# Q and K weights first on ScalarE's queue; Q projected once, its norm rows in a bank of their own

## The chip, the cores and the metric

The kernel runs on one core of one Trainium2 chip. The metric is device time in microseconds: the median of the runs of one program, lower is better. The profile comes from one further execution, which has a time of its own.

## The reference

There are two branches over the same sequence, mixed by a gate. One is softmax attention with 16 heads of 28 dimensions over 2048 tokens of width 448. The other is a spectral filter: a 2-D real FFT of x, a product with a complex weight, and the inverse FFT.

```python
def reference(A_x, A_wqkv, A_wo, B_x, B_w_r, B_w_i, gate_w):
    # A: qkv = x @ wqkv, 16 heads of 28; p = softmax(q k^T * 28**-0.5); a = (p v) @ wo
    # B: X = rfft2(x) over sequence and width; b = irfft2(X * (w_r + 1j * w_i))
    x = A_x                                            # [1, 2048, 448]
    g = _sigmoid((x * gate_w).sum(-1, keepdims=True))
    a = _A_ref(x, A_wqkv, A_wo)
    b = _B_ref(x, B_w_r, B_w_i)
    return g * a + (1 - g) * b
```

As the kernel computes it, both branches read the same x.

## The kernel before

The program is a list of operations (`Op`), each with an engine, an estimated duration, what it depends on and a key. A planner that ran beforehand put all of them into one order. That order is stored as the compressed constant `PLAN`, with the PSUM bank of each background item and a list of the operations that are moved to VectorE. `plan()` unpacks it and `issue()` emits the operations in that order, so the order of every engine's instructions, and of every queue's transfers, is fixed when the kernel is built. Each engine works through its instructions strictly in order. Numbers from 60000 up in the list stand for fillers: four matmuls over a tile of zeros into `pvb`, which change no result and which the planner puts where it expects TensorE to wait. PSUM has 8 banks: `psA` has three, `psB` two, `pvb` one, and `bg` two, which the background items share.

Attention works in 16 rounds (`plan_steps`): 4 groups of 4 heads, by 4 blocks of 512 queries. In each round the scores of a key tile are computed transposed, k by q, for four heads side by side. Most of them go through ScalarE's exponential (line 962), three units of 512 columns from `psA` and then two from `psB`, in turn, 307 times in all; `ring` keeps the results until `pvb` has summed them against the values. For the other key tiles, VectorE (line 997) and GpSimd or VectorE (line 1009, the phase operations) form the exponential from bits. The norms of q and k enter the scores as two more rows of q and k: a row with -0.5 times the sum of squares on one side stands against a row of ones on the other. The constants `selq` and `selk` pick those rows in a matmul over the squares in `sq`.

The FFT branch, the projections of later groups and the output run as background between the scores: the forward FFT, 16 products (`CS` and `Wg` are loaded for each), the inverse FFT and the output tiles.

The head (`head`, from line 499) is what must be done before the first scores. It loads the first 512 tokens of x in two halves of two tiles (`dx`, 224 KB each, into `xtok`) and the weights of group 0 of Q and K (`raws`, 98 KB each, into `X`). Two queues issue loads: SyncE's (SP) and ScalarE's (ACT). GpSimd prepares constants and the zero columns of the padded weights (`padset`); ScalarE copies the raw weights into them (`padcopy`, line 494). While x is on its way, `NWARM` = 14 matmuls over zeros keep TensorE busy. Then x is transposed in four chunks c of 112 columns, each in a PSUM bank of its own (psA, psB, pvb and a background bank), and evicted to `xT` (lines 555 and 557), psB by ScalarE and the others by VectorE. Each projection is four matmuls over these chunks.

Q's first block is projected twice, into psA (`qa`), from which the squares are taken, and into pvb (`qb`), to which the norm row is added (`mq`) before pvb is evicted as q. The squares of `qa` are shared: 320 columns on ScalarE (line 582), 192 on VectorE (lines 584 and 586). The eviction is shared as well: 256 columns on VectorE (line 595), 256 on ScalarE (line 593). For K, the first `KA` = 256 columns follow the same scheme (`ka`, `kb`, `mk`; evicted by VectorE, line 597), the other 256 come behind (`kc`, `kd`, `mc`). Where two engines read one bank, the layer that builds the program makes them do so in turn. All matmuls carry the helper's line, 417, and all transposes 425.

## Time and profile before

| | us |
|---|---|
| median of 3 runs | 386.98 (386.85 to 387.02) |
| profiled execution, its time | 387.57 |
| its span, first to last instruction | 385.8 |
| TensorE busy | 370.4 |
| ScalarE busy | 366.1 |
| VectorE busy | 339.9 |
| GpSimd busy | 226.1 |

Busy times are of the span. A busy TensorE need not be at its peak: matmuls overlap, and each counts until its modelled end, so two matmuls that start 0.2 us apart may each show 0.38. In the timeline a row gives the start, the duration, the engine, the line, the operation with output and input, and in brackets how long the engine was idle before and what ended that. Rows merge equal instructions that follow each other (x14); "128*113 128x128" are the weights and the moving operand. `X` is the tile of raw weights, `wpq` and `wpk` the padded weights of Q and K, `ring` the result of the exponential. SPq and ACTq are the engines' queues issuing transfers.

### The profile page before, as it was taken

To read this page: it belongs to the slowest core of one execution; us is meant where nothing else is said; L and a number is where in the kernel's file an instruction comes from. 1 tells how busy PE (TensorE), PEld (TensorE's weight loads), DVE (VectorE), ACT (ScalarE), POOL (GpSimd) and SP (SyncE) were. 2 spreads that over 40 slices of the span, in tenths; PEclk is the share of its full clock that TensorE was granted. 3 is DMA by queue.
4 is the path that set the end of the run, shared out by engine and by line. 5 is a ranking of instruction groups with operands and counts; after the bars stand their busy time and mean duration, and the time that the engine had idled before them with its cause. 6 is when DMAs were issued, how large, how long until landed. Compare 5 with 4: busy or idle time off the path is not lost.

```text
span 385.8 us, 12111 instructions
## 1 busy us (share of the span) xinstructions
PE 370.4 (96%) x4978; PEld 142.3 (37%) x4978; DVE 339.9 (88%) x559; ACT 366.1 (95%) x333; POOL 226.1 (59%) x235
## 2 busy tenths in 40 slices
PE   7999999999999999999899999999999999999996
PEld 4643323334343334333233334332334323333343
DVE  1768989998999999999999999999999999977534
ACT  3899999999999999999999999999999999999993
POOL 4133686344566677878796776766557853454500
PEclk9999999999999999999999999999999999999999
DMA  8451000001230013233323212211123120030211
GB/s 212 99 147 39 3 2 2 14 6 45 55 108 4 2 51 79 72 73 99 71 79 70 48 31 75 67 41 25 46 76 103 51 66 14 4 82 26 56 37 62
DMA packets 31811, 21.63 MB, mean 56 GB/s; under 512 B 16572, under 2 KB 29596, under 8 KB 31756
## 3 DMA queue, kind: packets, MB, share of 16 engines
q1 hardware_dynamic: 30876, 20.41, 20.5%
q8 instruction: 39, 0.64, 0.7%
q10 hardware_dynamic: 880, 0.44, 0.4%
q14 instruction: 16, 0.13, 0.1%
HBM read 14.97 MB, written 1.97 MB: 44 GB/s over the span
## 4 chain that ended last, share of the span: by engine, by line
PE 63%; DVE 17%; ACT 5%; DMA 5%; issue 4%; POOL 2%; SPq 1%; ACTq 0%; DVEq 0%; POOLq 0%
PE bg L417 29%; PE pvb L417 20%; DVE pd L997 7%; PE psA L417 7%; PE psB L417 6%; ACT ring L962 5%; DVE pd L1009 3%; DMA CS<-cCS 2%; DVE X L1301 2%; POOL pd L1009 1%; SPq L400 1%; DMA X<-in_A_wqkv_dram 1%; DMA xtok<-Ab 1%; DMA Rb<-rsc 1%; DVE tt L1258 1%
## 5 line engine op out<-in xcount | busy, mean ns | idle before, releaser
L962 ACT ACTIVATE ring<-psA 128x1536 bf16<-128x1536 f32 x154 | 228.8, 1486 | 4.2 <-PE psA L417 3.1
L1009 POOL TENSOR_SCALAR pd<-pd 128x2048 uint16<-128x2048 uint16 x83 | 157.1, 1901 | 81.8 <-DVE pd L1009 47.1
L962 ACT ACTIVATE ring<-psB 128x1024 bf16<-128x1024 f32 x153 | 162.5, 1062 | 2.1 <-PE psB L417 1.6
L997 DVE TENSOR_SCALAR pd<-bg 128x512 uint16<-128x512 f32 x236 | 156.0, 683 | 9.0 <-PE bg L417 5.1
L417 PE MATMUL bg<-q,k 32*128 32x512 bf16 x236 | 88.0, 379 | 3.4 <-DVE pd L997 0.9
L417 PE MATMUL pvb<-pd,vd 128*32 128x512 bf16 x944 | 85.5, 384 | 0.3 <-DVE pvs L1078 0.2
L417 PEld LDWEIGHTS <-k 32*128 32x128 bf16 x1024 | 37.4, 91 | 106.7 <-issue 100.6
L417 PE MATMUL pvb<-ring,vw 128*32 128x512 bf16 x768 | 71.1, 384 | 0.0
L1009 DVE TENSOR_SCALAR pd<-pd 128x2048 uint16<-128x2048 uint16 x94 | 65.7, 715 | 1.3
L417 PE MATMUL psA<-q,k 32*128 32x512 bf16 x474 | 64.1, 383 | 0.7 <-ACT ring L962 0.6
L417 PE MATMUL psB<-q,k 32*128 32x512 bf16 x314 | 62.4, 383 | 1.1 <-ACT ring L962 0.5
L417 PEld LDWEIGHTS <-vd 128*32 128x32 bf16 x944 | 22.9, 94 | 36.1 <-issue 31.1
L417 PEld LDWEIGHTS <-vw 128*32 128x32 bf16 x788 | 19.5, 94 | 31.4 <-issue 26.6
L1089 POOL TENSOR_TENSOR q<-pvs,Rb 128x512 bf16<-128x512 f32 x15 | 19.2, 1277 | 13.4 <-DVE pd L1009 5.2
L417 PEld LDWEIGHTS <-xT 112*128 112x128 bf16 (+1 forms) x512 | 19.6, 97 | 9.8 <-issue 6.4
L1258 DVE TENSOR_TENSOR tt<-bg,Wg 128x900 bf16<-128x900 f32 x16 | 17.4, 1091 | 2.0 <-PE bg L417 1.5
L417 PE MATMUL bg<-xT,wpk 112*32 112x512 bf16 (+2 forms) x252 | 18.3, 376 | 0.3 <-DVE pd L997 0.2
L875 POOL TENSOR_TENSOR vd<-vraw,wg 128x448 bf16<-128x448 f32 x16 | 15.0, 942 | 4.9 <-DVE pd L1009 4.2
L417 PE MATMUL bg<-xT,wpq 112*32 112x512 bf16 (+1 forms) x240 | 17.7, 382 | 0.2 <-DVE pd L997 0.2
L417 PE MATMUL bg<-wo,q 128*32 128x448 bf16 x236 | 17.5, 354 | 0.0
L1157 DVE CAST fin<-bg 128x448 bf16<-128x448 f32 x12 | 7.5, 624 | 10.8 <-PE bg L417 8.2
L417 PE MATMUL bg<-Bd,X 113*32 113x448 bf16 x240 | 16.8, 355 | 0.0
(125 smaller groups left out, 321.0 us busy)
## 6 DMA issues: line engine op xcount, KB each, us to landing
Rb<-rsc SPq DMA_DIRECT2D x60, 64.0 KB
CS<-cCS SPq DMA_DIRECT2D x16, 192.0 KB
Wg<-in_B_w_i_dram SPq DMA_DIRECT2D x64, 28.1 KB
xtok<-Ab SPq DMA_DIRECT2D x16, 112.5 KB
V<-xtok SPq DMA_DIRECT2D x16, 112.5 KB
xtok<-in_A_x_dram SPq DMA_DIRECT2D x3, 448.0 KB
out_dram<-fin SPq DMA_DIRECT2D x12, 112.0 KB
Wg<-in_B_w_r_dram SPq DMA_DIRECT2D x32, 28.1 KB
```

Source lines behind the costliest of these rows:

```text
L400: self.pin(e.dma_start(out=out() if callable(out) else out, in_=in_() if callable(in_) else in_))
L417: self.pin(self.nc.tensor.matmul(out, lhsT=lhsT, rhs=rhs, start=start, stop=stop, **kw))
L875: self.pin(nc.gpsimd.tensor_tensor(out=self.vd[g][:, f, :, :, 0:DH], in0=src, in1=wv, op=ALU.mult))
L962: self.pin(nc.scalar.activation(out=home[:, u0:u0 + len(st), :], in_=slot[:, 0:len(st), :], func=ACT.Exp, scale=LN2 / UNITS))
L997: self.pin(nc.vector.tensor_scalar(out=self.pd[y.bank][:, s, :].bitcast(U16), in0=self.bgi(it), scalar1=127 * UNITS, scalar2=0.0, op0=ALU. ...
L1009: self.pin(e.tensor_scalar(out=fl(self.pd[z.bank]), in0=fl(self.pd[y.bank]), scalar1=float(PHASE[f]), scalar2=1.0, op0=ALU.add, op1=ALU.mult))
L1089: e = self.pool(1.24, lambda: self.pin(nc.gpsimd.tensor_tensor(out=dst, in0=pvs[:], in1=self.Rb[:], op=ALU.mult)), ds, kk)
L1157: e = self.dve(0.55, lambda: self.pin(V.tensor_copy(out=fin, in_=bank())), [ops[-1], self.fdma[t % 2]], key, **a)
L1258: self.pin(nc.vector.tensor_tensor(out=tt[:], in0=free_dims(self.bgi(it), [[0, 2], [F, 2], [1, F]]), in1=free_dims(Wg[:], [[F, 2], [F, 2], ...
L1301: self.pin(nc.vector.tensor_tensor(out=free_dims(self.zt[0:FN], [[128, 4], [1, 128]], 512 * t), in0=self.bgi(it)[0:FN, :].rearrange("p (a ...
```

## The change

- ScalarE's queue issues Q's weights and then K's; SyncE's queue issues both halves of x. Before, each queue issued one half of x and then one of the two weights.
- The transposes of all four chunks of the first half of x stand ahead of those of the second half, and in the new order the last of them stand ahead of Q's projection.
- Q's first block is projected once, into psA. ScalarE evicts it to q with the scale CQ (`qc`); VectorE squares q in SBUF (`sq`); the norm rows go alone into pvb (`mq`, now opening its bank), and VectorE adds pvb to q in one operation (`qe`).
- ScalarE still squares the first 256 columns of K, and now also evicts them (`self.k0`). The other 256 columns stay on VectorE.
- The warm-up matmuls write another bank of psA.
- `PLAN` is new as a whole. What it makes of the order: TensorE has 12 warm-ups, the transposes of the first half for psB, a warm-up, psA, a warm-up, pvb, then the second half for psA, pvb and psB, four for the background bank, then `qa`, `ka`, `kb`, `mq`, `mk`, `kc`, three of `kd`, and the first scores; before, it had all 14 warm-ups, and the first matmul of `qa` stood ahead of the last two transposes. ScalarE has the copies of Q's weights, of psB's xT and of K's weights in the order as before, then `qc`, K's square, K's eviction and the first exponential. In the second pair of scores psA's now stand ahead of psB's. Behind the head the order is the same but for neighbours that swap; there are 11 fillers for 6, 93 phase operations on VectorE for 94 and 84 on GpSimd for 83. On SyncE's queue the large loads of raw weights for later groups stand behind two small loads of `wo`, of which one waits for GpSimd.

```diff
@@ -501,14 +501,14 @@
         self.grp = "head"
         K0 = -5000.0
         self.pad_ms, self.wready, self.d_x, self.xev, self.xtr = {}, {}, [], {}, []
-        dx = [self.dma(self.xtok[:, 2 * i:2 * i + 2, 0:D], self.x[:, 2 * i:2 * i + 2, :], (), K0, dur=0.48,
-                       lat=2.95, eng=("SP", "ACT")[i], kb=224) for i in range(2)]
+        dx = [self.dma(self.xtok[:, 2 * i:2 * i + 2, 0:D], self.x[:, 2 * i:2 * i + 2, :], (), K0 + i, dur=0.5,
+                       lat=3.2 + 0.4 * i, kb=224) for i in range(2)]
         self.d_x.append(dx)
         raws = {}
         for i, (w, off) in enumerate((("q", 0), ("k", D))):
             o = 2 * 4 * 336 + 448 * i
-            raws[w] = self.dma(free_dims(self.U[0:C], [[C, 4], [1, C]], o), self.wsrc(off, 0, C), (), K0 + 1,
-                               eng=("ACT", "SP")[i], dur=0.52, lat=3.4)
+            raws[w] = self.dma(free_dims(self.U[0:C], [[C, 4], [1, C]], o), self.wsrc(off, 0, C), (), K0 + i,
+                               eng="ACT", dur=0.52, lat=3.5)
         self.d_cst = self.dma(self.cst[:], nc.inline_tensor(small_consts(), name="ccst").ap(), (), K0 + 2, dur=0.55,
                               lat=3.9, kb=80)
         ms0 = self.pool(0.3, lambda: self.pin(nc.gpsimd.memset(self.zero[:], 0.0)), (), K0)
@@ -519,7 +519,7 @@
             out=self.ident[:], in_=self.ident[:], compare_op=ALU.is_equal, fill=0.0, base=0, pattern=[[-1, P]],
             channel_multiplier=1)), (idm,), K0 + 0.6)
         tl = self.act(1.35, lambda: self.pin(nc.scalar.activation(out=self.ge[:, 0:1], in_=self.zero[:, 0:1],
-                                                                  func=ACT.Exp)), (ms0, raws["q"]), K0 + 3)
+                                                                  func=ACT.Exp)), (ms0, raws["k"]), K0 + 3)
         tl.deps = [ms0]
         for i, w in enumerate("qk"):
             self.padset(w, 0, K0 + 2 + i)
@@ -530,22 +530,24 @@
         self.rawrd = self.wready["k", 0] + self.wready["q", 0]
         warm = []
         for i in range(NWARM):
-            warm.append(self.pe(0.213, lambda: self.mm(self.slots[0][:, 0, 0:256], self.zero[:, 0:P], self.zero[:], True,
+            warm.append(self.pe(0.213, lambda: self.mm(self.slots[0][:, 1, 0:256], self.zero[:, 0:P], self.zero[:], True,
                                                        True), (ms0,), K0 + i * .01))
 
         b0 = Item()
         homes = [lambda: self.psA[:, 0, :], lambda: self.psB[:, 0, :], lambda: self.pv[:], lambda: self.bgi(b0)]
         CO = (0, 2, 1, 3)
-        for j, c in enumerate(CO):
-            ops = []
-            for i in range(2):
+        trs = {}
+        for i in range(2):
+            for j, c in enumerate(CO):
                 def f(c=c, i=i):
                     for t in (2 * i, 2 * i + 1):
                         o = homes[c]().bitcast(BF16)[0:C + 1, P * t:P * t + P]
                         self.tr(o, self.xtok[:, t, C * c:C * c + C + 1])
                 a = dict(it=b0, first=i == 0) if c == 3 else {}
-                ops.append(self.pe(0.13, f, [dx[i], d_id, msx] + ops, K0 + 10 + 0.01 * i + j * .1, **a))
-            self.xtr += ops
+                trs[i, c] = self.pe(0.13, f, [dx[i], d_id, msx] + ([trs[0, c]] if i else []), K0 + 10 + i + j * .1, **a)
+        self.xtr += list(trs.values())
+        for j, c in enumerate(CO):
+            ops = [trs[0, c], trs[1, c]]
             eng = "ACT" if c == 1 else "DVE"
 
             def fe(c=c, eng=eng):
@@ -575,55 +577,44 @@
                                    ops[-1:] + warm[-1:] + list(deps), key + 0.1 * j, **d))
             return ops[-1]
 
-        def square(eng, src, o, n, deps, key, it=None):
-            i, d = o % 512, self.sq[:, o:o + n]
-            a = dict(it=it, rd=True) if it else {}
-            if eng == "ACT":
-                return self.act(0.19 + n / 1200.0, lambda: self.pin(nc.scalar.activation(
-                    out=d, in_=src()[:, i:i + n], func=ACT.Square)), deps, key, **a)
-            c = self.dve(0.1 + n / 960.0, lambda: self.pin(nc.vector.tensor_copy(out=d, in_=src()[:, i:i + n])), deps, key,
-                         **a)
-            return self.dve(0.06 + n / 1920.0, lambda: self.pin(nc.vector.tensor_tensor(out=d, in0=d, in1=d, op=ALU.mult)),
-                            (c,), key + 0.01, lk=True, name="sq")
-
-        def evict(eng, w, T, src, o, n, deps, key, it=None):
-            def f():
-                dst, s, z = T[:, o:o + n], src()[:, o:o + n], CQ if w == "q" else 1.0
-                if eng == "ACT":
-                    self.pin(nc.scalar.activation(out=dst, in_=s, func=ACT.Copy, scale=z))
-                elif w == "q":
-                    self.pin(nc.vector.tensor_scalar(out=dst, in0=s, scalar1=z, scalar2=None, op0=ALU.mult))
-                else:
-                    self.pin(nc.vector.tensor_copy(out=dst, in_=s))
-            return self.op(eng, (0.17 if eng == "ACT" else 0.12) + n / 1100.0, f, deps, key,
-                           **(dict(it=it, rd=True) if it else {}))
-
-        def addrow(w, bank, o, n, deps, key, **a):
+        def addrow(w, bank, o, n, start, deps, key, **a):
             i = o % 512
             return self.pe(0.217 * n / 512 + 0.01, lambda: self.mm(bank()[:, i:i + n], self.c("sel" + w), self.sq[:, o:o + n],
-                                                                   False, True), list(deps) + [self.d_cst], key, **a)
+                                                                   start, True), list(deps) + [self.d_cst], key, **a)
+
+        def mult(o, n, src, deps, key):
+            d = self.sq[:, o:o + n]
+            return self.dve(0.06 + n / 1920.0, lambda: self.pin(nc.vector.tensor_tensor(out=d, in0=src, in1=src, op=ALU.mult)),
+                            deps, key, lk=True, name="sq")
         q0, k0 = self.q[0], self.k[0]
         qa = proj("q", bqa, 0, 512, True, K0 + 20)
-        qb = proj("q", bqb, 0, 512, False, K0 + 20.05, [self.xev[0, 2]])
         ka = proj("k", bka, 0, KA, True, K0 + 21, it=b1)
-        kb = proj("k", bkb, 0, KA, False, K0 + 22.5, [self.xev[0, 1]])
-        sa = square("ACT", bqa, 0, 320, (qa, tl), K0 + 30)
-        sb = square("DVE", bqa, 320, 192, (qa,), K0 + 30)
-        sk = square("ACT", bka, 512, KA, (ka, tl), K0 + 31, b1)
-        mq = addrow("q", bqb, 0, 512, (sa, sb, qb), K0 + 22)
-        mk = addrow("k", bkb, 512, KA, (sk, kb), K0 + 23)
+        kb = proj("k", bkb, 0, KA, False, K0 + 21.5, [self.xev[0, 1]])
+        qc = self.act(0.17 + 512 / 1200.0, lambda: self.pin(nc.scalar.activation(out=q0[:, 0:512], in_=bqa(), func=ACT.Copy,
+                                                                                 scale=CQ)), (qa, tl), K0 + 30)
+        sk = self.act(0.19 + KA / 1200.0, lambda: self.pin(nc.scalar.activation(
+            out=self.sq[:, 512:512 + KA], in_=bka()[:, 0:KA], func=ACT.Square)), (ka, tl), K0 + 31, it=b1, rd=True)
+        sq = mult(0, 512, q0[:, 0:512], (qc,), K0 + 50)
+        mq = addrow("q", bqb, 0, 512, True, (sq, self.xev[0, 2]), K0 + 22)
+        mk = addrow("k", bkb, 512, KA, False, (sk, kb), K0 + 23)
         self.mk0 = mk
-        qe = [evict("DVE", "q", q0, bqb, 0, 256, (mq,), K0 + 50), evict("ACT", "q", q0, bqb, 256, 256, (mq,), K0 + 32)]
-        self.k0 = evict("DVE", "k", k0, bkb, 0, KA, (mk,), K0 + 51)
+        qe = self.dve(0.62, lambda: self.pin(nc.vector.scalar_tensor_tensor(
+            out=q0[:, 0:512], in0=bqb(), scalar=1.0 / CQ, in1=q0[:, 0:512], op0=ALU.mult, op1=ALU.add)), (mq, qc), K0 + 51)
+        self.k0 = self.act(0.17 + KA / 1200.0, lambda: self.pin(nc.scalar.copy(out=k0[:, 0:KA], in_=bkb()[:, 0:KA])), (mk,),
+                           K0 + 32)
         kc = proj("k", bkc, KA, 512, True, K0 + 24, [mk, mq], it=b2)
-        kd = proj("k", bkd, KA, 512, False, K0 + 25, [kc], it=b3)
-        sc = square("DVE", bkc, 512 + KA, 512 - KA, (kc,), K0 + 52, b2)
-        mc = addrow("k", bkd, 512 + KA, 512 - KA, (sc, kd), K0 + 28, it=b3, noext=True)
-        ke = evict("DVE", "k", k0, bkd, KA, 512 - KA, (mc,), K0 + 53, b3)
+        kd = proj("k", bkd, KA, 512, False, K0 + 25, [kc, sk], it=b3)
+        sr = self.sq[:, 512 + KA:1024]
+        sc = self.dve(0.07 + (512 - KA) / 960.0, lambda: self.pin(nc.vector.tensor_copy(out=sr, in_=bkc()[:, KA:512])),
+                      (kc,), K0 + 52, it=b2, rd=True)
+        sc = mult(512 + KA, 512 - KA, sr, (sc,), K0 + 52.1)
+        mc = addrow("k", bkd, 512 + KA, 512 - KA, False, (sc, kd), K0 + 28, it=b3, noext=True)
+        ke = self.dve(0.07 + (512 - KA) / 960.0, lambda: self.pin(nc.vector.tensor_copy(
+            out=k0[:, KA:512], in_=bkd()[:, KA:512])), (mc,), K0 + 53, it=b3, rd=True)
         self.sqrd = [mq, mk, mc]
-        self.qev[0, 0] = qe
+        self.qev[0, 0] = [qe]
         self.kev[0, 0] = [self.k0, ke]
-        self.pv0 = qe
+        self.pv0 = [qe]
 
 
     def weights(self):
```

More of the change, by code (lines that the diff above doesn't have):

```diff
@@ new lines @@
+        'Dw?XK5~!N0txBl6tE8%;s-@bgL~5K$p+>62Dw0a3lBiB9x$3M^snjZsN~zMRv?_y2uQI8Os;bJYqN^;by{e+Jsvatv%C2&#d@85P'
+        'rE;r0DzD0~3aEmrwrZ>jsiLZwDy)jDBC3QcsY<ERs;o+GQkrrqg{h;;sPbx#nycoi3TnPus1~WkYJpm!E~`}Lin^+<smZE|TB=f;'
+        'DJre0r_z|~YMENDR;ZP#zj~+Mt5vFn`k>O8(dwgGt<sy-@{d}hTB;0YfXZmrsy(Wj+N<`d{c4?BD+g3&vtCtKnanx0L7i6@)J3&j'
+        't&$yTr@EwesVpX|StGmEG&Nn#k{N2I>aCipY^IsYZU(77YO0#8`l^kpz8a+(s7<Panx%%Q9A>kcAzM^VQ&$aDTh%u8o2sFHS6$Q}'
+        'Dwp|F&5_*Zpt_-EN*<Hf98xz`R5`2~s#YqQZ={B)Tk43)XKt%W>W<29=E)aTz<gCJ<*xds3Yyj`nzT{()OR&jCHIBQeO1`3kRR%V'
```

123 lines of the change are left out of this document (59 added, 64 removed), and 20 rows, old and new, of the table PLAN.

## The prediction

> **What bounds the kernel now.** I read the page first: span and busy time, then the chain of work that ended last.
>
> ```profile
> span 385.8 us, 12111 instructions
> PE 370.4 (96%) x4978; PEld 142.3 (37%) x4978; DVE 339.9 (88%) x559; ACT 366.1 (95%) x333; POOL 226.1 (59%) x235
> PE 63%; DVE 17%; ACT 5%; DMA 5%; issue 4%; POOL 2%; SPq 1%; ACTq 0%; DVEq 0%; POOLq 0%
> ```
>
> TensorE and ScalarE are both busy for 95% or more, and the chain runs over TensorE for 63% of the span. Next come the busy times in stretches of 10 us; the columns are the stretch, its length, and the busy time of TensorE, weight loads, VectorE, ScalarE and GpSimd.
>
> ```profile
> 40.00:50.00 10.00, 10.00 (x138) 3.34 (x131) 9.66 (x17) 10.00 (x10) 7.30 (x6) 1.00 0.02 3
> 180.00:190.00 10.00, 8.85 (x124) 2.75 (x125) 9.44 (x15) 9.39 (x10) 8.21 (x7) 1.00 0.39 96
> ```
>
> In the first, TensorE has no gap; the second is its widest after the head, and still nearly full. So nearly all that follows the head is work standing in line, and starts when the head ends. What bounds the head is read from the timeline (start, duration, engine, line, operands).
>
> ```profile
> 0.80 0.48 ACTq L400 DMA_DIRECT2D xtok<-in_A_x_dram  x1
> 0.81 0.45 SPq L400 DMA_DIRECT2D xtok<-in_A_x_dram  x1
> 1.17 3.17 PE L417 MATMUL psA<-zero 128*128 128x256 bf16 x14 [1.17 <-POOL zero L514]
> 1.31 0.46 SPq L400 DMA_DIRECT2D X<-in_A_wqkv_dram  x1
> 1.31 0.51 ACTq L400 DMA_DIRECT2D X<-in_A_wqkv_dram  x1
> 4.46 0.30 PEld L425 LDWEIGHTS <-xtok 128*113 128x113 bf16 x4 [0.61 <-DMA xtok<-in_A_x_dram]
> 4.96 0.63 PEld L425 LDWEIGHTS <-xtok 128*113 128x113 bf16 x10 [0.19 <-DMA xtok<-in_A_x_dram]
> 5.12 0.39 PE L425 MATMUL pvb<-ident,xtok 128*113 128x128 bf16 x4
> 5.32 0.42 DVE L557 COPY xT<-psA 113x512 bf16<-113x512 bf16 x1 [5.32 <-PE psA L425]
> 5.34 0.28 PE L425 MATMUL psB<-ident,xtok 128*113 128x128 bf16 x2
> 5.66 0.41 DVE L557 COPY xT<-pvb 113x512 bf16<-113x512 bf16 x1
> 6.00 0.56 ACT L494 COPY wpq<-X 112x448 bf16<-112x448 bf16 x1 [2.65 <-DMA X<-in_A_wqkv_dram]
> 6.48 0.58 ACT L555 COPY xT<-psB 113x512 bf16<-113x512 bf16 x1
> 6.71 0.38 PE L417 MATMUL psA<-xT,wpq 112*128 112x512 bf16 x1 [0.99 <-ACT wpq L494]
> 6.95 0.57 ACT L494 COPY wpk<-X 112x448 bf16<-112x448 bf16 x1
> 7.24 0.42 DVE L557 COPY xT<-bg 113x512 bf16<-113x512 bf16 x1 [1.17 <-PE bg L425]
> 7.26 0.59 PE L417 MATMUL pvb<-xT,wpq 112*128 112x512 bf16 x2
> 8.02 0.38 PE L417 MATMUL psA<-xT,wpq 113*128 113x512 bf16 x1
> 8.44 0.36 DVE L584 CAST sq<-psA 128x192 bf16<-128x192 f32 x1 [0.77 <-PE psA L417]
> 8.83 0.44 ACT L582 ACTIVATE sq<-psA 128x320 bf16<-128x320 f32 x1 [1.31 <-DVE sq L584]
> 9.16 0.38 ACT L582 ACTIVATE sq<-bg 128x256 bf16<-128x256 f32 x1
> 9.31 0.38 PE L417 MATMUL pvb<-sq,cst 128*128 128x512 bf16 x1
> 10.17 0.42 DVE L597 CAST k<-psB 128x256 bf16<-128x256 f32 x1
> 10.19 0.38 ACT L593 ACTIVATE q<-pvb 128x256 bf16<-128x256 f32 x1 [0.65 <-DVE q L595]
> 10.65 0.39 PE L417 MATMUL psA<-q,k 32*128 32x512 bf16 x3
> 11.09 1.45 ACT L962 ACTIVATE ring<-psA 128x1536 bf16<-128x1536 f32 x1 [0.52 <-PE psA L417]
> 12.44 1.02 ACT L962 ACTIVATE ring<-psB 128x1024 bf16<-128x1024 f32 x1
> 14.17 1.45 ACT L962 ACTIVATE ring<-psA 128x1536 bf16<-128x1536 f32 x1 [0.53 <-PE psA L417]
> 15.94 0.43 DVE L780 TENSOR_TENSOR sq<-k 128x512 bf16<-128x512 bf16 x1
> 16.89 0.68 DVE L786 SCALAR_TENSOR_TENSOR k<-bg,k 128x512 bf16<-128x512 f32 x1
> ```
>
> x is there at 4.96, but ScalarE stands 2.65 us for Q's weights and copies them at 6.00. Its copy of xT follows at 6.48, the first projection starts at 6.71, and the last transposes, queued behind that projection, hold the last copy of xT until 7.24. So Q's projection ends at 8.40 (8.02 + 0.38): the late weights cost most. Then psA and pvb are each read by two engines in turn (8.44 and 8.83; the wait of 0.65 before 10.19). Scores start at 10.65, the first exponential at 11.09, the third only at 14.17.
>
> **The weights go first (part 1).** Each queue still issues two of these four loads, in the slots of 0.80 and 1.31. Q's weights take the slot in which half of x was first on ScalarE's queue. That half, 224 KB against 98, was used at 4.96; I put the weights at 4.7, between 4.46 (when the other half was used) and 4.96. Their copy ends near 5.3 instead of 6.56. K's weights, second on that queue, replace the load that was used at 6.00, behind 224 KB. Now only 98 KB lie ahead; needed at 6.25, they hide behind the copy of xT. The price is x's second half, second on SyncE's queue, issued about 0.45 late (the length of the issue at 0.81). Bounds: 4.96, if the lighter neighbour makes up for it, and about 6.4: the 6.00 at which a second load was used, and some 126 KB more, about 0.4 to 0.5. I take 5.25, nearer the low end, since half of x now shares the engines with 98 KB instead of with 224 KB. SyncE's later issues (constants, the next block of x) keep their places; the large weight loads behind them wait for a memset of wo and come some microseconds later, but their copies start only after 20 us:
>
> ```profile
> 20.61 0.56 POOL L496 COPY wpk<-X 112x448 bf16<-112x448 bf16 x1
> ```
>
>
> **The path from x to the first exponential (part 2).** Let x be complete at T = 5.25; T was 4.96. The first copy of xT starts at T+0.36 and the second at T+0.70, as now. psB's transposes now stand ahead of bg's, and all before the projection. ScalarE copies psB at T+0.53 = 5.78, with Q's weights done at 5.3, and K's weights 0.47 behind it, to 6.82. VectorE's third copy follows its second by 0.34, at 6.29, and ends at 6.71. The last of Q's four projections starts at 6.75 and ends at 7.13, against 8.40: a gain of 1.27.
>
> **The norm rows in their own bank (part 3).** Q's second projection, four matmuls with 512 columns, goes. Two of them take 0.59 at 7.26, of which 0.38 is the last one's latency: 0.21 each, 0.85 off TensorE. On the path, steps replace steps. ScalarE evicts 512 columns: 0.38 for 256 and 0.44 for 320 make 0.62, from 7.17 to 7.79. VectorE multiplies 512 columns in SBUF (0.43 at 15.94), 7.83 to 8.26. The row matmul (0.38 at 9.31) ends at 8.68, and the fused add (0.68 at 16.89) runs from 8.72 to 9.40. K's square is queued on ScalarE behind the eviction, 7.68 to 8.06, and K's eviction moves there, 8.83 to 9.21; both hide beside VectorE's add, with 0.2 to spare. Scores at 9.48, exponential at 9.92. From Q's projection to the scores that is 2.35 us, against 2.25 now: two waits for a bank go, and longer single operations replace them, so part 3 alone loses about 0.1 on this path. First exponential: 11.09 - 9.92 = 1.17 earlier.
>
> **The next two rounds (part 4).** Now psB's second scores stand ahead of psA's, and so wait for the exponential that ends at 13.46; psA's come behind them and the third exponential at 14.17. In the new order psA's come first. They need VectorE's square for the other half of K, one row matmul, half of the next block's transposes with a copy of xT, and four transposes of k. From 9.40 these add up to psA's scores near 11.9 and a third exponential near 12.4, 1.7 earlier than 14.17. I carry 1.6 into the stretches where TensorE is full; the bounds are 1.17 and 1.9.
>
> **The rest of the plan (part 5).** The new plan keeps the order behind the head but for neighbours that swap. Two things change in number: five more fillers of four matmuls, and one more phase operation on GpSimd, one fewer on VectorE.
>
> ```profile
> L417 PE MATMUL pvb<-zero x24: 272/272/283, 262.8 to 278.1; 128*32 128x256 bf16 x24
> L1009 POOL TENSOR_SCALAR pd<-pd 128x2048 uint16<-128x2048 uint16 x83 | 157.1, 1901 | 81.8 <-DVE pd L1009 47.1
> L1009 DVE TENSOR_SCALAR pd<-pd 128x2048 uint16<-128x2048 uint16 x94 | 65.7, 715 | 1.3
> PEld L417 <- DMA CS<-cCS: 2.0, 2, 1.1
> ```
>
> A filler streams 256 columns, half of a 0.21 matmul, its four parts side by side: five cost 0.55 at most, and nothing where TensorE waits anyway. I take 0.2, since they stand where ScalarE and VectorE have no gap. The moved phase is worth between -0.7 (VectorE gets its 715 ns back) and +1.2 (the result 1901 ns after the start instead of 715); I take 0, as GpSimd is idle 41% of the span. Waits for the constants CS, 1.1 at the longest, can go or come, because their loads move by a few places on SyncE's queue: 0, between -1.1 and +1.1.
>
> **Sum.** -1.6 + 0.2 = -1.4 on the profiled execution: its 387.57 (span 385.8, and 1.8 around it) becomes 386.2. That execution lies 0.6 above the median, 386.98, so for the median I forecast **385.6**.
>
> **Rivals.** (a) *The clock rises late.* The 14 warm-up matmuls start 0.21 apart (3.17 less the last one's 0.42, over 13) for 256 columns; at 7.26 the same time does 512. So TensorE runs at half speed at first; by 5.12 it is fast, since four transposes of 128 columns span 0.39, each 0.22 long, so 0.06 apart. In the new order 12 warm-ups end near 3.9 and it idles until x comes near 4.4, with the other two among the transposes. If that gap keeps the clock low for a second stretch as long as the first (from 1.17 to somewhere between 4.34 and 5.12), ten transposes cost 0.05 more each up to the last copy, 0.5, and the last of Q's matmuls come 0.5 later still: about 1.0 in all. Time 386.6. The granted clock reads 1.00 throughout and so cannot tell; three runs within 0.17 us speak against a clock that is on the brink. [...] (b) *x comes late*, at 6.4 rather than 5.25: 1.15 later throughout, -1.4 + 1.15: 386.7. Against it: a second load came by 6.00 behind as many bytes. (c) *The lead is lost behind the head*, in a stage set by loads and not by TensorE: 387.0, no change. For it: the gaps at 180 to 190; against it: the loads shift with the work that releases them. (d) *Slower.* Near scores 277 to 279, two phases of one key block go from VectorE to GpSimd, one behind the other. If the sum over values stands for each on TensorE's queue, which is in order, all scores behind it wait: 2 x 1.2 = 2.4 against the gain of 1.4, so 388.0. It decides once these stalls pass 1.4 us. Against it: GpSimd has much free time there, and VectorE gets other phases back.
>
> **How the numbers follow.** Forecast 0.60, with its own range 384.5 to 386.4 (the -1.1 of CS below, a lead of 1.17 with the fillers at 0.55 above). Rivals (a) 0.12, (b) 0.08, (c) 0.08, (d) 0.12. A measurement of this kernel tells about 0.2% from no change, 0.77 us: faster means below 386.2. The forecast gives faster 0.57 and same 0.03, mild cases of (a) and (b) faster 0.05, the rest of them and (c) same 0.23, (d) slower: 0.62, 0.26 and 0.12. Range 384.5 to 387.1, which leaves out (d).
>
> **What would show it.** Right: ScalarE's first copy of weights near 4.7, x's last transposes near 5.25, Q's projection done near 7.1, first exponential near 9.9, the third near 12.4, and the same lead when the last exponential ends. Wrong: that copy after 5.5, or x after 6 (part 1); transposes 0.1 apart after 5 (a); a lead of 1.5 at the third exponential that is gone at the end (c, d).

## The result, and the profile after

Twenty-two executions of each kernel on one chip gave a median of 385.72 us for the changed kernel (385.15 to 386.35) and 386.86 us for the kernel before (385.9 to 391.74): a ratio of 0.9968 (95% interval 0.9955 to 0.9981), 1.14 us. The profiled execution of the changed kernel took 386.27 with a span of 384.5, 1.3 less than before. On two other chips the same pair gave 0.9948 (0.9925 to 0.9972) and 0.9941 (0.9910 to 0.9972). Why the gain differs so much is told below.

The page of the changed kernel: span, busy times, and the chain of work that ended last.

```profile
span 384.5 us, 12127 instructions
PE 369.8 (96%) x4994; PEld 143.6 (37%) x4994; DVE 337.8 (88%) x556; ACT 367.1 (95%) x333; POOL 229.1 (60%) x236
PE 56%; DVE 18%; ACT 14%; issue 5%; DMA 3%; SPq 2%; POOL 0%; DVEq 0%; ACTq 0%; POOLq 0%
```

The busy times have hardly moved. The chain still runs mostly over TensorE. The time went from the places where TensorE was not busy, first of all from the head. Its timeline:

```profile
0.80 0.99 ACTq L400 DMA_DIRECT2D X<-in_A_wqkv_dram  x2
0.81 1.04 SPq L400 DMA_DIRECT2D xtok<-in_A_x_dram  x2
1.17 2.74 PE L417 MATMUL psA<-zero 128*128 128x256 bf16 x12 [1.17 <-POOL zero L514]
4.12 0.56 ACT L494 COPY wpq<-X 112x448 bf16<-112x448 bf16 x1 [0.81 <-POOL wpk L481]
4.33 0.46 PE L425 MATMUL psB<-ident,xtok 128*113 128x128 bf16 x2 [0.42 <-DMA xtok<-in_A_x_dram]
5.45 0.42 PE L425 MATMUL psA<-ident,xtok 128*113 128x128 bf16 x2
5.66 0.42 PE L425 MATMUL pvb<-ident,xtok 128*113 128x128 bf16 x2
6.07 0.39 PE L425 MATMUL bg<-ident,xtok 128*113 128x128 bf16 x4
6.27 0.58 ACT L557 COPY xT<-psB 113x512 bf16<-113x512 bf16 x1 [1.58 <-PE psB L425]
6.38 1.14 PE L417 MATMUL psA<-xT,wpq 112*128 112x512 bf16 x4
7.56 0.60 ACT L593 ACTIVATE q<-psA 128x512 bf16<-128x512 f32 x1 [0.24 <-PE psA L417]
8.19 0.43 DVE L587 TENSOR_TENSOR sq<-q 128x512 bf16<-128x512 bf16 x1 [1.20 <-ACT q L593]
9.08 0.69 DVE L601 SCALAR_TENSOR_TENSOR q<-pvb,q 128x512 bf16<-128x512 f32 x1 [0.47 <-PE pvb L417]
9.85 0.39 PE L417 MATMUL psA<-q,k 32*128 32x512 bf16 x3
10.29 1.45 ACT L953 ACTIVATE ring<-psA 128x1536 bf16<-128x1536 f32 x1 [0.73 <-PE psA L417]
11.64 1.02 ACT L953 ACTIVATE ring<-psB 128x1024 bf16<-128x1024 f32 x1
12.71 0.39 PE L417 MATMUL psB<-q,k 32*128 32x512 bf16 x2
12.76 1.45 ACT L953 ACTIVATE ring<-psA 128x1536 bf16<-128x1536 f32 x1
```

Q's weights are copied at 4.12 instead of 6.00 (there the last thing that ScalarE waited for was a memset of GpSimd, no longer the load), and the projection starts at 6.38 and ends at 7.52. The first exponential starts at 10.29, 0.80 earlier; the third at 12.76, 1.41 earlier. Two things are new to the eye. The pairs of transposes at 5.45 and 5.66 stand 0.21 apart, 0.105 for each, while in the profile before four of them took 0.39 with their latency: here TensorE was still at half speed until about 6.1. And the lead is not constant behind the head, as this table shows. It gives how much earlier the n-th exponential starts than in the profile of before, in us (minus: later). The kernels of the other columns follow below.

| n (from 0) | changed | changed, third profile | load of CS put back | old head, load of CS moved |
|---|---|---|---|---|
| 0 | 0.80 | 0.98 | 0.92 | -0.01 |
| 2 | 1.41 | 1.58 | 1.52 | -0.64 |
| 4 | 1.11 | 1.28 | 1.22 | -0.64 |
| 8 | 1.02 | 1.20 | 1.13 | -0.64 |
| 60 | 0.48 | 0.66 | 0.59 | -0.64 |
| 132 | 0.86 | 1.39 | 1.31 | -0.56 |
| 140 | 0.46 | 0.99 | 0.92 | -0.56 |
| 146 | 1.41 | 1.94 | 0.36 | -0.11 |
| 197 | 1.01 | 1.75 | 0.09 | -0.15 |
| 198 | 1.59 | 2.34 | 0.68 | 0.44 |
| 306, the last | 1.48 | 2.24 | 0.58 | 0.26 |

So the head gives about 1.0 us by the eighth exponential, some of it fades, and between the 132nd and the 146th another 0.55 comes in. A third step, 0.59 at the 198th, is in all four columns, also in that of the old head, and in every other profile of this study: it belongs to the one profile of before. Only there TensorE's matmuls wait at that place for a load of CS:

```profile
250.17 0.57 PE L417 MATMUL bg<-xtok,CS 128*32 128x450 bf16 x12 [0.56 <-DMA CS<-cCS]
```

That execution took 387.57, 0.59 above the median that was known then. So the lead at the end, 1.48, holds 0.59 that the change did not earn.

The second place, between the 132nd and the 146th, lies near 185 us. Rows of SyncE's queue and of TensorE there, first before, then changed:

```profile
180.01 0.59 SPq L400 DMA_DIRECT2D Bd<-cBinv  x1
182.00 0.53 SPq L400 DMA_DIRECT2D CS<-cCS  x1
186.43 0.57 PE L417 MATMUL bg<-xtok,CS 128*32 128x450 bf16 x12 [0.85 <-DMA CS<-cCS]
```

```profile
180.79 0.54 SPq L400 DMA_DIRECT2D CS<-cCS  x1
181.37 0.57 SPq L400 DMA_DIRECT2D k<-nrow  x1
184.88 0.56 PE L417 MATMUL bg<-xtok,CS 128*32 128x450 bf16 x12
```

Before, TensorE stands 0.85 us for a load of CS (192 KB). Ahead of that load the queue has a load of 448 KB for Bd and a transfer of a row of k. In the new plan both stand behind it, the load is issued earlier relative to the work, and the wait is gone. Nothing in the change's words speaks of this place; it is a by-product of the new plan. That only neighbours swap behind the head does not hold on SyncE's queue: the load of Bd stood three transfers ahead of that load of CS and now stands eight behind it (issued at 180.01, now at 186.12).

### The profile page after: what moved, and what is told of

Read it like the earlier page. It is cut to its first block, busy times and chain, and to the rows that moved or that the text cites. A ratio compares the mean times of both kernels' runs of the same rounds, so it can differ in the third digit from the quotient of the medians.

```text
span 384.5 us, 12127 instructions
## 1 busy us (share of the span) xinstructions
PE 369.8 (96%) x4994; PEld 143.6 (37%) x4994; DVE 337.8 (88%) x556; ACT 367.1 (95%) x333; POOL 229.1 (60%) x236
## 4 chain that ended last, share of the span: by engine, by line
PE 56%; DVE 18%; ACT 14%; issue 5%; DMA 3%; SPq 2%; POOL 0%; DVEq 0%; ACTq 0%; POOLq 0%
PE bg L417 27%; PE pvb L417 16%; ACT ring L953 14%; DVE pd L988 7%; PE psA L417 7%; PE psB L417 5%; DVE pd L1000 2%; DVE X L1292 2%; SPq L400 2%; DVE tt L1249 1%; PE bg L425 1%; DMA xtok<-Ab 1%; DVE sq L724 1%; DMA xtok<-in_A_x_dram 1%; DVE X L1198 1%
## 5 line engine op out<-in xcount | busy, mean ns | idle before, releaser
L1000 POOL TENSOR_SCALAR pd<-pd 128x2048 uint16<-128x2048 uint16 x84 | 158.9, 1898 | 81.9 <-DVE pd L1000 40.3
L1000 DVE TENSOR_SCALAR pd<-pd 128x2048 uint16<-128x2048 uint16 x93 | 63.7, 701 | 1.3
L417 PE MATMUL psB<-q,k 32*128 32x512 bf16 x314 | 63.3, 383 | 1.1 <-ACT ring L953 0.8
L417 PEld LDWEIGHTS <-xT 112*128 112x128 bf16 (+1 forms) x512 | 19.6, 97 | 10.3 <-issue 6.7
```

The source lines that it names most:

```text
L417: self.pin(self.nc.tensor.matmul(out, lhsT=lhsT, rhs=rhs, start=start, stop=stop, **kw))
L1000: self.pin(e.tensor_scalar(out=fl(self.pd[z.bank]), in0=fl(self.pd[y.bank]), scalar1=float(PHASE[f]), scalar2=1.0, op0=ALU.add, op1=ALU.mult))
```

## The experiments

Three groups ran, each on one chip beside runs of the kernel before, whose medians there were 387.84, 388.29 and 388.93. Absolute times are compared within a group only. Each kernel ran 5 to 12 times in its group, and one execution of it was profiled. Edits that add lines shift the line numbers of the rows below by some places.

### The clock in the head: warm-ups with and without the gap

The changed kernel again (its second profile), a version with all 14 warm-ups first, one with 17, and that with x's second half shared by both queues.

```diff
-        return [int(i) if i >= 60000 else self.ops[i] for i in order]
+        order = [int(i) if i >= 60000 else self.ops[i] for i in order]
+        warm = [o for o in order if not isinstance(o, int) and o.name == "warm"]
+        i = order.index(warm[0])
+        rest = [o for o in order if isinstance(o, int) or o.name != "warm"]
+        return rest[:i] + warm + rest[i:]
```

(17: the first three of these emit two matmuls each.) For the last one:

```diff
+        def x1():
+            for t, e in ((2, nc.sync), (3, nc.scalar)):
+                self.pin(e.dma_start(out=self.xtok[:, t:t + 1, 0:D], in_=self.x[:, t:t + 1, :]))
```

> The changed kernel once more, beside the three that follow. Both theories: ratio to the kernel before near 0.997, first exponential at 10.3, the third at 12.8; half of x seen complete near 5.2 and used at 5.45. Its lead over the kernel before at each later exponential, set beside the first profile's, shows how far two executions of one program drift apart behind the head; I expect 0.2 to 0.4 us.

> All 14 warm-up matmuls ahead of the first transposes, as before the change; nothing else. Theory (the idle stretch from 3.9 to 4.3 kept the array at half speed until about 6.0, as in rival (a)): the array is fast by 4.7, the transposes of x's second half start at 5.28 and lie 0.06 apart, first exponential near 9.9, 0.3 to 0.4 earlier than in the changed kernel, and the total 0.3 less. Rival (when the array becomes fast does not hang on that gap): transposes still 0.11 apart until about 6, and only the two warm-ups that stood between them are won: first exponential near 10.1.

> 17 warm-ups (three more), all ahead of the transposes, so that no gap is left before x comes: they end near 4.8, and the six transposes of x's first half need 0.33 more, to 5.15, before the second half is there at 5.2. Theory: fast from about 4.6 on, first exponential near 9.9 as with 14, or earlier than with 14 if the remaining gap of 0.2 mattered. Rival (half speed lasts for a set time whatever the warm-ups do): transposes 0.11 apart until 6 and first exponential 10.2 or later.

> As with 17 warm-ups, and x's second half is issued as two tiles of 112 KB, one behind x's first half on SyncE's queue, the other on ScalarE's queue between Q's weights and K's. Theory (x's second half now sets the head, and Q's weights come more than a microsecond too early): x complete near 4.9 instead of 5.2, first exponential near 9.55, total 0.3 less than with 17 warm-ups. Rival (the engines' total bandwidth sets when all four loads are in, whatever their order): x complete at 5.1 to 5.2 still, K's weights later, first exponential near 9.9.

Measured: 386.22, 385.68, 385.61 and 386.14 us, ratios 0.9948 (0.9925 to 0.9972), 0.9947 (0.9932 to 0.9962), 0.9942 (0.9927 to 0.9957) and 0.9959 (0.9945 to 0.9973). The intervals overlap; no version is told from another. The profiles say more. TensorE's transposes in the changed kernel again, and with 17 warm-ups:

```profile
4.49 0.32 PE L425 MATMUL psB<-ident,xtok 128*113 128x128 bf16 x2 [0.58 <-DMA xtok<-in_A_x_dram]
4.76 0.27 PE L425 MATMUL psA<-ident,xtok 128*113 128x128 bf16 x2
5.46 0.32 PE L425 MATMUL psA<-ident,xtok 128*113 128x128 bf16 x2 [0.20 <-DMA xtok<-in_A_x_dram]
10.20 1.45 ACT L953 ACTIVATE ring<-psA 128x1536 bf16<-128x1536 f32 x1 [0.73 <-PE psA L417]
```

```profile
1.17 3.81 PE L421 MATMUL psA<-zero 128*128 128x256 bf16 x17 [1.17 <-POOL zero L518]
5.41 0.42 PE L429 MATMUL psA<-ident,xtok 128*113 128x128 bf16 x2
5.62 0.42 PE L429 MATMUL pvb<-ident,xtok 128*113 128x128 bf16 x2
10.29 1.45 ACT L959 ACTIVATE ring<-psA 128x1536 bf16<-128x1536 f32 x1 [0.73 <-PE psA L421]
```

The first has a gap of 0.58, and its transposes are fast from the first pair on (0.27 for a pair, where a slow one shows 0.42). The second has no gap, and is slow past 5.62, to about 6.2. So the gap did not decide when the clock rose. (With 14 warm-ups, also without a gap, it rose near 5.1, and the first exponential came at 9.86, as the theory had it; with 17 at 10.29, as the rival had it.) Over all profiles of this study it rose near 3.8, by 3.95, by 4.5 (three times), near 5.1, near 6.1 to 6.2 (four times), near 6.5 (twice), near 8.3 and near 10.3. The last two had gaps of 0.63 and 0.33 in front; what sets it was not settled. The spread is over 6 us, over kernels whose first matmul falls at 1.17 in all, and 1.6 us (by 4.5 to near 6.1) between profiles of one and the same kernel.

Sharing x's second half helped the head (TensorE waits for the last of x until 4.94, first exponential at 9.70) and not the median.

The changed kernel again shows how far two executions of one program drift apart: its three profiles end with leads of 1.48, 0.96 and 2.24 over the profile of before, where 0.2 to 0.4 apart was expected.

### Parts of the head

(1) The old kernel with the new assignment of queues; (2) the changed kernel with the old one; (3) the changed kernel with the second scores in the old order; (4) the changed kernel without fillers.

```diff
 (1) -                        lat=2.95, eng=("SP", "ACT")[i], kb=224) for i in range(2)]
     +                        lat=2.95, kb=224) for i in range(2)]
     -                                eng=("ACT", "SP")[i], dur=0.52, lat=3.4)
     +                                eng="ACT", dur=0.52, lat=3.4)
 (2) the reverse of (1), and the load of x's second half ahead of Q's weights in the order
 (3) +        a, b = [order.index(self.scores[i]) for i in (2, 3)]
     +        order.insert(a, order.pop(b))
 (4) -        return [int(i) if i >= 60000 else self.ops[i] for i in order]
     +        return [self.ops[i] for i in order if i < 60000]
```

(In (1) the first pair of lines is the two halves of x, which go to SyncE's queue, and the second the two weights.)

> The kernel before, with the assignment of the two queues alone changed: Q's and K's weights on ScalarE's queue, both halves of x on SyncE's; its plan is otherwise the old one. Theory (the late weights held the head): ScalarE copies Q's weights near 4.2 instead of 6.00, the first projection starts near 6.1 instead of 6.71, Q's projection ends 7.4 to 7.8 instead of 8.40, the first exponential starts at 10.1 to 10.5 instead of 11.09, and the total falls by 0.5 to 0.8 us. Rival (the gain comes from the new plan of the head, not from the queues): the first exponential stays within 0.3 of 11.1 and the total within 0.3 us of the kernel before.

> The changed kernel with the old assignment of the queues: half of x first on ScalarE's queue and Q's weights behind it, K's weights behind the other half on SyncE's. The norm rows, the order of the transposes and of the second scores stay new. Theory (the weights are worth most, the new plan part of it): Q's weights are copied near 6.0, Q's projection ends near 7.7 to 8.0, the first exponential starts at 10.4 to 10.8, and the total lies 0.3 to 0.7 us above the changed kernel. Rival (all of the head's gain is the weights'; the norm path by itself loses 0.1): first exponential at 11.1 to 11.2, total as the kernel before.

> The changed kernel with its second scores in the old order, psB's ahead of psA's. Theory (TensorE's chain is gated by the end of the second exponential, which frees psB, whichever scores come first): the third exponential starts near 13.4 instead of 12.76, but the fifth and later ones within 0.2 of the changed kernel, and the total within 0.3 us of it. Rival (the prediction: what the third exponential gains is carried to the end): every later exponential 0.5 to 0.6 later, the total 0.5 to 0.6 us above the changed kernel.

> The changed kernel without all 11 of its filler matmul groups (each four matmuls of 256 columns side by side, into a bank that nobody reads). Theory (a filler takes TensorE's time where it stands on the path, and 0.11 us at most): the total falls by 0.2 to 0.8 us, 1.2 at the very most, and the granted clock stays at 1.00. Rival 1 (they stand where TensorE waits anyway): no change within 0.2 us. Rival 2 (they keep TensorE's clock up): the granted clock falls below 0.99 somewhere and the total rises by over 0.5 us.

Measured, in one group: (1) 388.08, ratio 0.9991 (0.9957 to 1.0025); (2) 386.42, 0.9952 (0.9931 to 0.9974); (3) 386.08, 0.9945 (0.9923 to 0.9967); (4) 387.23, 0.9970 (0.9947 to 0.9994).

(1) and (2) are a poor measure of the weights, because of the clock. In the profile of (1) Q's weights are copied at 4.27, as its theory had it, yet the first exponential comes at 12.67; in (2) they are copied at 6.01 and it comes at 11.35. TensorE of (1) in the head:

```profile
6.35 0.42 PE L425 MATMUL bg<-ident,xtok 128*113 128x128 bf16 x2
9.55 0.63 PE L417 MATMUL pvb<-xT,wpq 112*128 112x512 bf16 x1
10.56 0.38 PE L417 MATMUL pvb<-xT,wpq 113*128 113x512 bf16 x1
12.67 1.45 ACT L962 ACTIVATE ring<-psA 128x1536 bf16<-128x1536 f32 x1 [0.52 <-PE psA L417]
```

A matmul of 512 columns takes 0.63 at 9.55 and 0.38 at 10.56: half speed until about 10.3. When the clock rose in the eleven other executions of each is not known. By the medians (2) lies 0.34 above (3), which has the weights first, and the intervals overlap. The last group gives a second measure. What (1) showed instead is the place near 185 us. Below are stretches of 2 us of its profile; the columns are the stretch, its length, the busy times of TensorE, weight loads, VectorE, ScalarE and GpSimd, then the granted clock.

```profile
188.17 0.94 PE L417 MATMUL bg<-xtok,CS 128*32 128x450 bf16 x12 [1.13 <-DVE pd L1009]
185.00:187.00 2.00, 1.78 (x19) 0.31 (x11) 2.00 (x5) 2.00 (x3) 2.00 (x3) 1.00 0.46 127
187.00:189.00 2.00, 0.87 (x16) 0.29 (x12) 1.14 (x2) 1.33 (x2) 0.94 (x2) 0.75 0.21 35
189.00:191.00 2.00, 2.00 (x20) 0.60 (x20) 1.69 (x2) 1.24 (x1) 2.00 (x2) 0.50 0.21 38
191.00:193.00 2.00, 2.00 (x23) 0.29 (x11) 0.48 (x1) 0.67 (x2) 0.58 (x2) 0.50 0.25 45
193.00:195.00 2.00, 2.00 (x19) 0.35 (x23) 1.07 (x3) 1.93 (x2) 0.45 (x2) 0.55 0.08 13
195.00:197.00 2.00, 2.00 (x39) 0.91 (x43) 1.93 (x4) 1.48 (x3) 0.30 (x1) 1.00 0.10 10
```

```profile
187.75:188.00 0.25, 0.00 (x0) 0.00 (x0) 0.25 (x1) 0.25 (x1) 0.00 (x0) 0.96 0.52 76
188.00:188.25 0.25, 0.08 (x4) 0.08 (x8) 0.17 (x1) 0.25 (x1) 0.00 (x0) 0.50 0.18 42
```

TensorE stands 1.13 us for the same load of CS: the row of its matmul names VectorE, but its weight loads, which start at the same 188.17, had waited 1.43 for CS. The granted clock halves at about 188.0, some 0.95 us into that gap, as shorter stretches show, and comes back at about 194.8. From 189 to 195 TensorE has no idle time at all; the 156th exponential starts 3.1 us later against before than the 132nd did. Half a clock for 6.8 us is a mean of 0.991 over the span of 389.7, the mean that this execution shows. A mean of 0.996 would be about 3.1 us at half clock, an estimate by the same sum; no profile shows one. The other executions show such means too: of 84 executions of the kernel before in the three groups, 43 have a mean clock of 0.998 or more (median 387.4), 28 one of 0.994 to 0.996 (389.1) and 13 one of 0.987 to 0.991 (390.6). Of the 46 of the changed kernel, none is below 0.998. (The clocks of the 22 executions of before on the first chip are not known.) The clock is not the whole gain. Among executions with a mean clock of 0.998 or more, the median of the changed kernel lies 1.5 below that of before in the first group (386.22 against 387.74) and 0.8 in the third (385.95 against 386.72). Even at that clock the executions of before spread from 385.88 to 389.88; why was not traced.

(3) decides for its theory in the main, against the prediction's carried lead. The third exponential starts at 13.56, 0.80 later than in the changed kernel, and the first 0.20 later (its transposes were slow until about 6.6). From n = 5 to 116 they are 0.40 to 0.43 later (behind that the two profiles part once more, which was not traced): 0.41 - 0.20 = 0.21 is what the order of the second scores is worth, not 0.6. (4): exponentials 0 to 116 lie a constant 0.46 ahead of the changed kernel's, the head's own difference; up to the 239th, where most fillers are behind, they are never over 0.47 ahead, so taking them out gained nothing, and the median is 0.8 and 1.15 above (2) and (3). The granted clock of all its executions is 0.998 or more. So the fillers show no cost, and no execution without them shows a low clock. Near the end of this profile GpSimd waits 4.78 us for a broadcast (Rb) instead of 3.50 and the last exponentials come 0.5 later; whether the fillers' absence causes that was not shown.

### The load of CS, and the head without it

The kernel that runs unchanged here gives the third profile of the changed kernel.

```diff
+        cs = [o for o in d if o.grp == "fc5" and o.kb == 192][0]
+        late = [o for o in d if o.grp == "fcst" and o.kb == 448][-1:] + [o for o in d if o.grp == "kg2"][3:4]
+        order = [o for o in order if o not in late]
+        i = order.index(cs) + 1
+        return order[:i] + late + order[i:]
```

That is for the old kernel (d is the list of its transfers). The changed kernel gets the reverse: its two such transfers ahead of that load. The old kernel with both has the edit above and that of (1).

> The kernel before, with two transfers on SyncE's queue (448 KB of Bd and one row of k) moved behind the load of CS that TensorE waits for near 185 us; its head is the old one. Theory (part of the changed kernel's gain comes from there: in the old order TensorE stands idle for 0.85 to 1.1 us at that load, and in a part of the executions the granted clock halves for some microseconds behind it): the idle time there falls below 0.4 us, no execution has a mean granted clock below 0.998, the median falls by 0.8 to 1.7 us against the kernel before on the same chip, and the lowest times by 0.3 to 0.6. Rival (all of the gain is the head's): median within 0.3 us of the kernel before, and mean clocks of 0.990 to 0.996 in as many executions as there.

> The changed kernel with the same two transfers put ahead of that load of CS, as in the kernel before; its head stays new. Theory: TensorE waits 0.5 to 1.1 us for CS near 184 us, a part of the executions has a mean granted clock of 0.990 to 0.996, and the median rises by 0.4 to 1.5 us against the changed kernel on the same chip. Rival (the head's gain alone counts): within 0.2 us of the changed kernel, clock 0.998 or more throughout.

> The changed kernel once more, beside the others on the same chip. Both theories: a ratio of 0.994 to 0.997 to the kernel before, with no mean clock below 0.998; the first exponential starts at 9.7 to 10.4, by when the clock has risen.

> The kernel before with both: the two transfers behind the load of CS, and Q's and K's weights on ScalarE's queue with x on SyncE's. The old plan of the head (norm rows over two projections, banks read by two engines) stays. Theory (the load of CS and the weights make the gain, the rest of the new head little): the median within 0.5 us of the changed kernel, and a first exponential near 10.3 where the clock rises by 6 us. Rival (the new plan of the head is needed): 0.6 us or more above the changed kernel.

Measured beside 35 executions of the kernel before (median 388.93):

| kernel | median, us | ratio, 95% interval | executions with a mean clock of 0.996 or less |
|---|---|---|---|
| before | 388.93 | | 19 of 35 |
| old head, load of CS moved | 386.93 | 0.9963 (0.9929 to 0.9996) | 2 of 12 |
| the same, and weights first | 386.53 | 0.9963 (0.9932 to 0.9993) | 0 of 12 |
| changed, load of CS put back | 387.27 | 0.9970 (0.9937 to 1.0003) | 4 of 12 |
| changed | 385.94 | 0.9941 (0.9910 to 0.9972) | 0 of 12 |

In the old kernel with the load moved, and in the changed kernel with it put back, TensorE at that place reads:

```profile
185.96 0.56 PE L423 MATMUL bg<-xtok,CS 128*32 128x450 bf16 x12
```

```profile
185.92 0.31 PEld L423 LDWEIGHTS <-CS 128*32 128x32 bf16 x12 [1.81 <-DMA CS<-cCS]
185.92 0.57 PE L423 MATMUL bg<-xtok,CS 128*32 128x450 bf16 x12 [1.32 <-DMA CS<-cCS]
```

The wait goes with the one edit and comes with the other, 1.32 us long; the lead of the kernel with the load put back falls from 1.31 to 0.36 between the 132nd and the 146th exponential, though the clock stayed at 1.00 in that profile. The four executions with a clock of 0.996 took 388.99 to 389.07, the others 385.67 to 387.60. So the theory holds in its main point: the order of these transfers makes the wait, and with the wait low clocks become frequent (19 of 35 against 2 of 12, 4 of 12 against 0 of 12). That the clock falls inside the wait was seen in one profile only, that of (1). Three numbers of the theory for the old kernel were missed: two executions still had a low clock, the median fell by 2.0 instead of 0.8 to 1.7, and the lowest time did not fall (386.31 against 385.88).

What the wait costs without the clock is less sure. By the leads it is 0.45 in the old kernel (0.56 late before the place, 0.11 late behind it). In the changed kernel it is 1.5: with the load put back 0.94 is lost, where the third profile, 0.08 ahead of it until then, gains 0.55. But among executions with a clock of 0.998 or more 0.7 in the changed kernel (386.65, eight, against 385.95, twelve) and nothing in the old one (386.85, ten, against 386.72, sixteen). So by the medians the 2.0 us there came with the clock. The two executions with a low clock of the old kernel with the load moved were not profiled, and what lowered their clock is open; its profile also lost 0.64 at the third exponential to a late load of another block of x, which the table of leads shows.

The head's own gain, with the load of CS in its new place, is 386.93 - 385.94 = 1.0 us: 0.4 when the weights go first (386.93 to 386.53), 0.6 with the new plan of the head (386.53 to 385.94). The profile of the kernel with both edits starts its first exponential at 10.88 with the clock rising near 6.5. Its 0.59 above the changed kernel lies between the theory (within 0.5) and the rival (0.6 or more). The split is smaller than the spread of the single executions, and by the spans, from first to last instruction, it turns round: their medians are 385.15, 384.5 and 384.2, so 0.65 for the weights and 0.3 for the plan. The rest lies outside the span: the old kernel with the weights first spends 2.0 to 2.2 us there in each of its 24 executions, in (1) and here, every other kernel 1.7 to 1.9. What that is was not traced. The sum of 1.0 agrees with the lead of 1.0 to 1.2 at the eighth exponential.

## Why the prediction was right, point by point

The forecast was 385.6 with a range from 384.5 to 387.1; the median is 385.72.

**Part 1 (weights first)** was right in kind. The copy started at 4.12, 4.33 and 4.41 in three profiles of the changed kernel, below the lower bound of 4.46. x's first half, on the other queue, was taken up at 4.33, 4.49 and 4.07, so neither load is always the first. x's second half was taken up at 5.46 where TensorE waited for it and at 5.19 in the third profile, for 5.25.

**Part 2 (Q's projection)** was to end at 7.13 and ended at 7.52 in the profile after. The missing 0.4 is half speed: the transposes of x's first half and the two warm-ups among them ran without a pause up to 5.45, and the second half's at 0.1 each instead of 0.06. Where the clock had risen in time, the working holds: from x's second half to the first exponential 5.46 to 10.20 = 4.74 in the second profile, against 5.25 to 9.92 = 4.67 predicted.

**Part 3 (norm rows)** was right: from the projection's end to the scores 9.85 - 7.52 = 2.33, predicted 2.35.

**Part 4 (the next two rounds)** is the term that was mis-sized: the carried lead. The third exponential came at 12.76, for 12.4, 1.41 earlier than before, and the prediction carried 1.6 on. But by the sixth only 1.02 was left, 1.2 with the faster head of the third profile; the bound below was 1.17. The step that failed is that the third exponential marks the start of the full stretch. psB's second scores wait in either order for the second exponential, which frees psB (they start at 13.51 before and at 12.71 after, 0.05 behind its end in both), and TensorE's queue goes on behind them. So what is carried is the lead of the second exponential, 0.80, plus the 0.21 that the order gives.

**Part 5 (the rest)** took fillers at 0.2; without them nothing was gained. It took the waits for CS at 0 between -1.1 and +1.1, and this term came out about half way to its lower bound: the step near 185 us is 0.55 in each of the three profiles of the changed kernel. The profile of before had shown the wait, and the prediction's row names two, 2.0 us in all. The second is gone in every other profile, with the old order too, so it is no gain of the change. And the new order behind the head was put at nothing, though it costs: every profile with the new plan loses 0.53 to 0.55 of its lead between the eighth and the 60th exponential, also without fillers, and none with the old plan does. Why was not traced. The prediction knew that these loads move by a few places and did not work out which way. What it had no thought of is the clock: it read 1.00 in that one profile of before and was taken for constant, while 41 of the 84 later executions of the kernel before had a mean clock of 0.996 or less, by the estimate above 3.1 us or more at half clock.

So the number came out close by luck, because errors of opposite sign met: 0.4 to 0.6 too much from the head and 0.5 too little taken off for the new order behind it, on the one side; about 0.5 too little from CS, and more where the clock fell, on the other. Set beside the profile of before, 0.59 more comes from that execution alone; the prediction had allowed for this when it took 0.6 off to come from that execution to the median.

**Rivals.** (a), the clock rising late, happened in two of three profiles of the changed kernel, by about 1.6 us later than in the profile of before, at a price of about 0.2 to 0.4 instead of the 1.0 worked out (0.4 on Q's projection in the profile after; in the third, 10.11 - 5.19 = 4.92 from x's second half, against 4.74). Its mechanism, the gap behind 12 warm-ups, fell: without any gap, with 17 warm-ups, the clock rose as late (near 6.2). (b): x was not late. (c) happened in part: the lead shrank from 1.02 to 0.48 by the 60th exponential, and most of what came back later came at the two places where before waits for CS. (d): no stall of 2.4 us shows; from the 144th exponential to the last the lead stays within 0.8 to 1.6 in the profile after.

## What to carry over

A short wait of a full engine can cost more than its length, when the granted clock falls in it, as in (1), where 1.13 us of waiting and 6.8 us at half clock went with 3.1 us of lead: read the mean clock of every execution, not only of the profiled one, and when part of them is lower, look for the longest idle time of TensorE. When a plan is rebuilt, compare the order on the DMA queues around every wait that the old profile shows, also far from the edit; here two transfers that changed places gave a step of 0.55 us between the two profiles, and more between the medians. Before a step in a lead is put down to a change, see whether kernels without that change show it too: 0.59 of the lead here was an accident of the one profile of before. Carry a head's lead from the point where the engine that is full later stops waiting for the other one, not from the earliest instruction that gained most.

## What the runs showed of the hardware

In the profile of (1) TensorE's granted clock fell to one half about 0.95 us into a gap of 1.13 us, in a stretch in which TensorE was otherwise nearly always busy (1.78 of the 2 us ahead of it), and stayed low for about 6.8 us (188.0 to 194.8) although TensorE was busy again from 188.17 on; in the profiles of before and of the changed kernel with the load of CS put back, a gap of 0.85 and one of 1.32 us at the same place left it at 1.00. With warm-ups that start at 1.17 in every profile, TensorE left half speed anywhere between 3.8 and 10.3 us, and between 4.5 and 6.1 in three profiles of one and the same kernel; and the granted clock in the records reads 1.00 in every stretch up to 16 us of the five profiles for which it was read there, that of (1) among them, so only the distances between matmuls show it (0.21 us between matmuls of 256 columns at half speed, 0.11 behind it).
